# Matmuls on zeros in TensorE's idle time at the start of a fused recurrence and highway layer

## The chip, the cores and the metric

The kernel runs on one core of a Trainium2 chip. The metric is the device time of one execution in microseconds (us), the median over several runs. The core has five engines that run side by side: TensorE (PE in the profile, its weight loads PEld), VectorE (DVE), ScalarE (ACT), GpSimd (POOL) and SyncE (SP), which here only issues DMAs.

## The reference

The inputs are x and f_logit, 4 x 6336 x 256 in float32, and the weights of a highway layer of width 256. A gated recurrence runs along the 6336 steps of each batch, and its result passes the highway layer, token by token:

```python
sig = 1.0 / (1.0 + np.exp(-f_logit))
f = lower_bound + (1.0 - lower_bound) * sig
i = 1.0 - f
for t in range(S):
    h = f[:, t] * h + i[:, t] * x[:, t]
    y[:, t] = h

H = np.maximum(y @ w_h, 0.0)
T = 1.0 / (1.0 + np.exp(-(y @ w_t + b_t)))
out = T * H + (1.0 - T) * y
```

## The kernel before

The 25344 tokens are cut into 25 units: 24 of 1024 tokens of one batch and a last one that holds the rest of all four batches. A unit has eight blocks of 128 tokens. The front part of a unit (up to the recurrence) is worked in pieces, `fronts`. The first unit is cut into pieces of two, two and four blocks, the second, the third and the last into four and four; the others are one piece. The back part (the highway layer) is worked in `backs`, mostly whole units.

For the recurrence the channels must lie on the partitions and time along the row, so the front part transposes. Each step has a letter:

- L and X load a piece of f_logit (tile `lt`) and of x (tile `xt`), both issued by SP. Q loads the weights.
- U (ACT, L154) makes `u`, the sigmoid of minus f_logit, with tokens on partitions.
- P (POOL, L160) multiplies u by x into `bv`, two blocks at a time.
- A (PE, L198) transposes u into PSUM (`uT`), one 128x128 matmul a block and half of the channels. F (ACT, L205) makes the decay `f` of it, one half of the channels at a time.
- B (PE, L215) transposes bv into PSUM (`bT`), two packed bf16 values as one float32.
- S (DVE, L230) is the scan of one half of the channels over the piece, the recurrence itself. It writes `y`, from which the next piece of the same batch continues.
- W (DVE, L148) scales the weights into `w_sb`, once, in two halves.

The back part: Z and G (PE, L245) are the two products of y with the weights, `zp` and `gp`; T (ACT, L251) is the sigmoid of zp, D (DVE, L256) the maximum; E (DVE, L166) and H (POOL, L160) multiply the two into `e`; O (PE, L296 and L297) brings the sum back to tokens on partitions; C (ACT, L303) and V (DVE) copy it out of PSUM into `o`; R (SP) stores it.

The order of all this work is one string, `PLAN`, written out by hand. The loop at the end takes letter after letter and issues that step's next instance; after A, B, Z, G and O a digit names the PSUM slot. Every instruction is pinned to this order on its engine, so each engine works its own list strictly in order, and semaphores join the lists. Transposes (A and B) share two PSUM slots of one bank each, one0 and one1. Z, G and O share three slots of two banks each, two0, two1 and two2. A step whose slot is still being read waits for the reader.

Before the plan starts, DVE waits for the small load of `lb` (lower_bound), makes the constants cc and ncc (L135, L137) and, with identity matrices that POOL builds, some diagonal matrices. TensorE has nothing to do until the first u is there.

The plan before begins as follows. Its first A is the first instruction of TensorE.

```python
"XLLLXXLXLQQUUA0A1PFFFUFUB0PSSB1A0FFPSSPB1A0XLLXLXXPFUFSSWWPB1A0G0Z1PFFUPSSDPXLLXLB0A1G2Z0..."
```

Of the kernel before, what the change touches and what calls it, by code (L numbers as in the profile page):

```python
# [11 lines left out]
FP32 = mybir.dt.float32  # L12
BF16 = mybir.dt.bfloat16
# [6 lines left out]
def kernel(  # L20
# [16 lines left out]
    nc = tc.nc  # L37
    B, S, D = x.shape
    assert D == 256
    P = 128  # L40
    NH = D // P
    NB = 8
# [37 lines left out]
    singles = ctx.enter_context(tc.tile_pool(name="singles", bufs=1))  # L80
# [4 lines left out]
    def new(key, shape, dtype):  # L85
        return pools[key].tile([P, *shape], dtype, tag=key, name=key)

    def pin(ins):
        return tc.keep_in_program_order(ins)
# [12 lines left out]
    def load(i, name, src):  # L102
        u, j0, j1 = fronts[i]
        np_, j = units[u][0], run(fronts[i])
        t = fs[i][name] = new(name, [NB, D], FP32)
        pin(nc.sync.dma_start(t[:np_, :j1 - j0].rearrange("p (k j) d -> p k (j d)", j=j), tokens(src, u, j0, j1, j)))
# [6 lines left out]
    def shape(piece):  # L113

        u, j0, j1 = piece
        return units[u][0], j1 - j0

    lb = singles.tile([P, NH], FP32, name="lb")
    bt = singles.tile([P, NH], FP32, name="bt")
# [4 lines left out]
    def load_weights(k):  # L124
        pin(nc.sync.dma_start(w_raw[:, 1 - k], (moe_w_t, moe_w_h)[k].rearrange("(h p) o -> p h o", p=P)))
# [25 lines left out]
    def gate(i):  # L151
        np_, nb = shape(fronts[i])
        u = fs[i]["u"] = new("u", [NB, D], FP16)
        pin(nc.scalar.activation(u[:np_, :nb], fs[i]["lt"][:np_, :nb], AF.Sigmoid, scale=-1.0))  # L154
# [13 lines left out]
    def product(i, k, mul):  # L168
        np_, _ = shape(fronts[i])
        if "bv" not in fs[i]:  # L170
            fs[i]["bv"] = new("bv", [NB // 2, D, 2], BF16)
        mul(inner(fs[i]["bv"][:np_, k:k + 1])[:, 0], fs[i]["u"][:np_, 2 * k:2 * k + 2],
            fs[i]["xt"][:np_, 2 * k:2 * k + 2])
# [9 lines left out]
    def psum(slot, shape, key, dtype):  # L183
        tag = ("one" if dtype in (FP16, BF16) else "two") + slot
        return ps1.tile([P, *shape], dtype, tag=tag, name=key)
# [126 lines left out]
    def each(pieces, count):  # L312
        return [(i, k) for i, piece in enumerate(pieces) for k in range(count(piece))]

    def halves_of(pieces):
        return each(pieces, lambda p: len(halves(p)))
# [7 lines left out]
    kinds = {  # L324
        "L": (lambda i, _: load(i, "lt", f_logit), each(fronts, lambda p: 1)),
        "X": (lambda i, _: load(i, "xt", x), each(fronts, lambda p: 1)),
        "Q": (lambda i, k: load_weights(k), [(0, 0), (0, 1)]),
        "U": (lambda i, _: gate(i), each(fronts, lambda p: 1)),
        "P": (lambda i, k: product(i, k, gpsimd_mul), [p for p in products if p not in EARLY]),
        "p": (lambda i, k: product(i, k, vector_mul), [p for p in products if p in EARLY]),  # L330
        "A": (decay_pe, halves_of(fronts)),
        "F": (decay_act, each(fronts, lambda p: NH)),
# [14 lines left out]
    }  # L347

    PLAN = (
        "XLLLXXLXLQQUUA0A1PFFFUFUB0PSSB1A0FFPSSPB1A0XLLXLXXPFUFSSWWPB1A0G0Z1PFFUPSSDPXLLXLB0A1G2Z0PUTFFTPPB1S"  # L350
        "SDUSSEZ1A0G0G2A1DDPFTFFPPZ1A0B1O0O2PSSTFECCUB0Z1B1G0G2SDSDA0Z0TUFTPPPPPPA0G1B1FXLLLXRRXLXDESA0Z0Z2O1"
        "UFTCTB0G0A1O1O2SDPPPFCCB1A0Z1G0O2FTUCB0G1PPPHPSDSEDPA1Z0Z2B0O1FTUCTESA1G0G1B0DDHPPPPSZ2O0O1FUTCCB1SA"
        "0G2Z0B1FDUTPHPPSXXLRLRRRLRXLRRZ1A0G2O0PDTFCEEG1B1A0O2O0UFCCDSG1B0A1Z2Z0SDPHPPPPFTTA1B0O2O1G0HPSFCCZ2"
        "B1A0Z1DUTFTEG0O2PSPLXXRXRRRRDPPHCB1SA0O1G0Z2B1FCUTDEPSG1Z0A0O2FTCPDPPHB1A0Z1G0O2SFTCDEB0Z1A1G0PLLXRR"
        "RRSDPPPUFTO2B0A1Z0G1SHDCFTEO2B0G0Z1A1PPPPCUFTSDHO2B0A1G0Z1SCFTO2B0A1DEPSZ1G0PPPCUFTDHO2B0A1O0G1SCFCD"
        "EZ2B0A1Z0PSTFTPPPG1B1O2A0O0DUCFCSG1Z2A1B0HDELXLLRXRLLRXRRRRRXPSTFPPZ1G0O2B1DTCSZ1G2A0O0PHUFTCDEB1A0G"
        "2Z1O0PSPFTCDPPHB0G1G2A1Z0UFTSA0B1FDEDSPO1O0Z2B0PPCCTPHSO1A1G0Z2B0UFTCDEPSA1G0Z2O1PPDB0FTCSA1Z2G0O1PH"
        "FUCTDELXRRXXRRLRLXXRRRA1B0G0Z1PSFTO2DCB1A0G1Z0O2PPPHSUFCTDEB1A0Z1G2O0PSDFTCB0A1Z1G2SFPPPHDO0B1A0G2ET"
        "UCFPSO1PZ0CDTB1A0Z1G2SFTUHO0A0B1DFG1EPPPPSO2A0CCZ0DFB1O2Z1B0TCUTSESHPPG0A1Z2G1DDRRRRRRRRFFTA1B0O2Z0Z"
        "1FCFSEHTTG2B1G0O1RSDDCO2SRHCZ0G1STRO2TDDEZ0CTERTG1O2O0DVDVCO2CREVO1CRO0RCVRR"  # L360
    )
    assert all(PLAN.count(k) == len(places) for k, (_, places) in kinds.items())
    todo = {k: iter(places) for k, (_, places) in kinds.items()}
    letters = iter(PLAN)
    for k in letters:
        kinds[k][0](*next(todo[k]), *([next(letters)] if k in "ABZGO" else []))
# [1 line left out]
_INS = ['x', 'f_logit', 'lower_bound', 'moe_w_h', 'moe_w_t', 'moe_b_t']  # L368
# [26 lines left out]
```

## Time and profile before

| | us |
|---|---|
| median of 6 runs | 214.68 (214.33 to 214.90) |
| the profiled execution, its own time | 214.64 |
| its span, first to last instruction | 212.9 |
| first matmul starts | 6.71 |
| first scan starts | 9.34 |
| busy: PE, DVE, ACT, POOL | 188.1, 195.3, 193.7, 160.8 |

The profile is of one execution. Its span leaves 1.7 us of the execution's own time outside. Times in its views count from the span's start. A timeline row gives start, duration, engine, line, operation, output and inputs, shape and count; in brackets stands how long the engine had idled before and what ended that. Matmuls are pipelined and each row of them contains the time for the last result to arrive, so the pace of a group is read from the starts. The page's slices are a fortieth of the span each, 5.3 us, and their digits are busy tenths. The row PEclk is the clock that the throttle granted to TensorE.

### The profile page before, as it was taken

The page shows a single profiled execution, that of the slowest core. Times are in us where ns is not written, and L with a number is a line of the kernel's source. Part 1 is how long each engine was busy: PE and PEld are TensorE (multiplying, and loading weights), DVE is VectorE, ACT ScalarE, POOL GpSimd, SP SyncE. Part 2 cuts the span into 40 slices and gives each one's busy share as a digit, 9 for nine tenths or more (in the row PEclk, how much of TensorE's full clock was granted, in tenths as well). Part 3 has the DMA queues.
Part 4 walks back from the last instruction along what each step waited for, and adds up shares of the span by engine and source line. Part 5 has one row for each costly group of instructions (what it writes and reads, how often), then busy time and mean ns, then how long its engine had stood idle before and what let it go on. Part 6 is the DMA issues. An engine that isn't in the chain of part 4 may idle for free.

```text
span 212.9 us, 4616 instructions
## 1 busy us (share of the span) xinstructions
PE 188.1 (88%) x1800; PEld 131.9 (62%) x1800; DVE 195.3 (92%) x154; ACT 193.7 (91%) x194; POOL 160.8 (76%) x133
## 2 busy tenths in 40 slices
PE   0368988899898999999999999999999999999980
PEld 0245655468565767666766776668576676866770
DVE  1269999999999999999999999999999999999980
ACT  2757899999999999999999999999999999998750
POOL 4485745979499698978988988898898886866500
PEclk9999999999999999999999999999999999999997
DMA  4999999999999999999999999999999996252466
GB/s 96 402 411 431 422 426 428 423 422 422 422 422 416 423 420 423 430 420 416 428 420 426 423 426 425 424 410 427 417 429 405 357 394 258 85 213 99 195 250 200
DMA packets 17350, 78.69 MB, mean 370 GB/s; under 512 B 2352, under 2 KB 2864, under 8 KB 11952
## 3 DMA queue, kind: packets, MB, share of 16 engines
q1 hardware_dynamic: 16784, 78.39, 90.3%
q8 instruction: 14, 0.23, 0.4%
q10 hardware_dynamic: 544, 0.00, 0.1%
q14 instruction: 8, 0.07, 0.1%
HBM read 52.43 MB, written 25.95 MB: 368 GB/s over the span
## 4 chain that ended last, share of the span: by engine, by line
DMA 41%; ACT 20%; PE 18%; DVE 9%; issue 8%; POOL 1%; SPq 1%; ACTq 1%; DVEq 0%; POOLq 0%
DMA out_dram<-o 19%; DMA xt<-in_x_dram 18%; ACT t L251 6%; ACT u L154 5%; PE zp L245 5%; ACT f L205 5%; DMA lt<-in_f_logit_dram 4%; PE gp L245 4%; DVE d L256 4%; DVE y L230 4%; ACT o L303 4%; PE bT L215 3%; PE uT L198 2%; PE op L296 2%; PE op L297 1%
## 5 line engine op out<-in xcount | busy, mean ns | idle before, releaser
L160 POOL TENSOR_TENSOR bv<-u,xt 128x512 bf16<-128x512 f16 (+1 forms) x100 | 114.5, 1177 | 32.2 <-DVE e L166 10.3
L230 DVE TENSOR_TENSOR_SCAN y<-f,y,bT 128x1024 bf16<-128x1024 f16 (+3 forms) x56 | 106.5, 1919 | 2.9 <-ACT f L205 1.3
L205 ACT ACTIVATE f<-uT,ncc 128x1024 f16<-128x1024 f16 (+3 forms) x60 | 66.0, 1111 | 2.5 <-PE uT L198 2.5
L251 ACT ACTIVATE t<-zp,bt 128x1024 bf16<-128x1024 f32 (+1 forms) x52 | 63.8, 1249 | 1.0 <-PE zp L245 0.7
L256 DVE SCALAR_TENSOR_TENSOR d<-y,ncc,gp 128x1024 bf16<-128x1024 bf16 (+1 forms) x52 | 62.4, 1210 | 0.3 <-issue 0.2
L245 PEld LDWEIGHTS <-w_sb 128*128 128x128 f16 x400 | 38.0, 99 | 37.6 <-issue 5.8
L303 ACT COPY o<-op 128x1024 f32<-128x1024 f32 (+2 forms) x50 | 55.7, 1158 | 4.2 <-PE op L297 2.2
L154 ACT ACTIVATE u<-lt 128x2048 f16<-128x2048 f32 (+3 forms) x30 | 53.3, 1780 | 5.2 <-DMA lt<-in_f_logit_dram 5.2
L245 PE MATMUL zp<-y,w_sb 128*128 128x512 bf16 (+1 forms) x200 | 51.3, 382 | 1.0 <-DVE d L256 0.6
L245 PE MATMUL gp<-y,w_sb 128*128 128x512 bf16 (+1 forms) x200 | 51.3, 382 | 0.8 <-ACT t L251 0.2
L296 PE MATMUL op<-diag,y 128*128 128x128 f16 (+1 forms) x400 | 49.2, 219 | 1.9 <-DVE d L256 0.7
L160 POOL TENSOR_TENSOR e<-d,t 128x1024 bf16<-128x1024 bf16 x21 | 44.9, 2136 | 7.4 <-DVE e L166 2.6
L297 PE MATMUL op<-ident_b,e 128*128 128x128 bf16 (+1 forms) x400 | 49.2, 219 | 0.0
L297 PEld LDWEIGHTS <-e 128*128 128x128 bf16 (+1 forms) x400 | 44.8, 114 | 5.6 <-issue 3.4
L296 PEld LDWEIGHTS <-y 128*128 128x128 bf16 (+1 forms) x400 | 44.8, 114 | 2.7
L198 PE MATMUL uT<-ident_h,u 128*128 128x128 f16 (+1 forms) x400 | 32.1, 226 | 10.0 <-ACT u L154 7.2
L198 PEld LDWEIGHTS <-u 128*128 128x128 f16 (+1 forms) x400 | 27.3, 101 | 17.1 <-ACT u L154 7.5
L215 PE MATMUL bT<-ident_f,bv 128*128 128x128 f32 (+1 forms) x200 | 32.5, 285 | 5.1 <-DVE y L230 2.4
L215 PEld LDWEIGHTS bT<-ident_f,bv 128*128 128x128 f32 (+1 forms) x200 | 23.2, 146 | 11.8 <-issue 4.7
L166 DVE TENSOR_TENSOR e<-d,t 128x1024 bf16<-128x1024 bf16 (+2 forms) x26 | 19.0, 736 | 0.1
L230 DVE TENSOR_TENSOR_SCAN y<-f,bT 128x512 bf16<-128x512 f16 (+2 forms) x8 | 10.5, 1337 | 3.8 <-PE bT L215 3.8
L135 DVE TENSOR_SCALAR cc<-lb 128x2 f32<-128x2 f32 x1 | 0.2, 169 | 4.5 <-DMA lb<-in_lower_bound_dram 4.5
(19 smaller groups left out, 10.9 us busy)
## 6 DMA issues: line engine op xcount, KB each, us to landing
out_dram<-o SPq DMA_DIRECT2D x48, 512.0 KB, 13.5
lt<-in_f_logit_dram SPq DMA_DIRECT2D x21, 1024.0 KB, 14.7
xt<-in_x_dram SPq DMA_DIRECT2D x21, 1024.0 KB, 15.2
lt<-in_f_logit_dram SPq DMA_DIRECT2D x5, 512.0 KB, 8.1
xt<-in_x_dram SPq DMA_DIRECT2D x5, 512.0 KB, 8.2
lt<-in_f_logit_dram SPq DMA_DIRECT2D x2, 384.0 KB, 13.1
xt<-in_x_dram SPq DMA_DIRECT2D x2, 384.0 KB, 11.3
xt<-in_x_dram SPq DMA_DIRECT2D x2, 256.0 KB, 5.0
```

Source lines behind the costliest of these rows:

```text
L154: pin(nc.scalar.activation(u[:np_, :nb], fs[i]["lt"][:np_, :nb], AF.Sigmoid, scale=-1.0))
L160: ins = pin(nc.gpsimd.tensor_mul(out_, a, b))
L198: pin(nc.tensor.transpose(uT[:, j * np_:(j + 1) * np_], fs[i]["u"][:np_, j, h * P:(h + 1) * P], ident_h[:np_, :np_]))
L205: pin(nc.scalar.activation(f[:, :N].rearrange("p (k q j) -> p k q j", q=np_, j=j), fs[i]["uT", h].rearrange("p (k j q) -> p k q j", q=np_, ...
L215: pin(nc.tensor.transpose(t[:, k // r, k % r], fs[i]["bv"][:np_, k, h * P:(h + 1) * P].rearrange("p d j -> p (d j)").bitcast(FP32), ident_ ...
L230: pin(nc.vector.tensor_tensor_scan(y, fs[i]["f", h][:, c:c + w], fs[i]["bT", h][:, c:c + w], 0.0 if prev is None else prev, op0=ALU.mult, ...
L245: pin(nc.tensor.matmul(p[:, a:e], w_sb[:, k, ki, h * P:(h + 1) * P], y_of(j)[:, ki, a:e], start=ki == 0, stop=ki == NH - 1))
L251: pin(nc.scalar.activation(bs[j]["t"][:, m, :width(backs[j])], bs[j]["zp", m], AF.Sigmoid, bias=bt[:, m:m + 1]))
L256: pin(nc.vector.scalar_tensor_tensor(bs[j]["d"][:, m, :width(backs[j])], y_of(j)[:, m], ncc[:, m:m + 1], bs[j]["gp", m], op0=ALU.mult, op1 ...
L296: pin(nc.tensor.matmul(o, y[:, h, cols], diag[:, h], start=True, stop=False))
L297: pin(nc.tensor.matmul(o, bs[j]["e"][:, h, cols], ident_b, start=False, stop=True))
L303: pin(copy(bs[j]["o", q][:np_, a:e], bs[j]["op", q][:np_, a:e]))
```

## The change

A tile `filler` of 128x512 bf16 is set to zero by DVE ahead of all else. A new letter M in the plan stands for one matmul of 128x512 that takes its weights and its moving data from filler and writes into a PSUM tile `busy`, which takes slot two2 ahead of that slot's other users. Nobody reads busy. 22 letters M are put into the head of the plan: 11 before the first A, one after each of the first two A, four after the first B, and five before the third B. All other letters keep their order, and so does every engine's list of the other instructions.

```diff
+    filler = singles.tile([P, 512], BF16, name="filler")
+    nc.vector.memset(filler, 0.0)
 
     lb = singles.tile([P, NH], FP32, name="lb")
...
-        "XLLLXXLXLQQUUA0A1PFFFUFUB0PSSB1A0FFPSSPB1A0XLLXLXXPFUFSSWWPB1A0G0Z1PFFUPSSDPXLLXLB0A1G2Z0PUTFFTPPB1S"
...
+        "XLLLXXLXLQQUUMMMMMMMMMMMA0MA1PFFFUFUMB0PSSMMMMB1A0FFPSSPMMMMMB1A0XLLXLXXPFUFSSWWPB1A0G0Z1PFFUPSSDPXL"
+        "LXLB0A1G2Z0PUTFFTPPB1SSDUSSEZ1A0G0G2A1DDPFTFFPPZ1A0B1O0O2PSSTFECCUB0Z1B1G0G2SDSDA0Z0TUFTPPPPPPA0G1B1"
...
+    assert set(PLAN) <= {*kinds, *"M012"}
     assert all(PLAN.count(k) == len(places) for k, (_, places) in kinds.items())
     todo = {k: iter(places) for k, (_, places) in kinds.items()}
+    busy = psum("2", [NB * P], "busy", FP32)
     letters = iter(PLAN)
     for k in letters:
+        if k == "M":
+            pin(nc.tensor.matmul(busy[:, :512], filler[:, :P], filler, start=True, stop=True))
+            continue
         kinds[k][0](*next(todo[k]), *([next(letters)] if k in "ABZGO" else []))
```

More of the change, by code (lines that the diff above doesn't have):

```diff
@@ L349 @@
     PLAN = (
-        "XLLLXXLXLQQUUA0A1PFFFUFUB0PSSB1A0FFPSSPB1A0XLLXLXXPFUFSSWWPB1A0G0Z1PFFUPSSDPXLLXLB0A1G2Z0PUTFFTPPB1S"
[L351 to L359, printed above, removed]
@@ L360 @@
-        "1FCFSEHTTG2B1G0O1RSDDCO2SRHCZ0G1STRO2TDDEZ0CTERTG1O2O0DVDVCO2CREVO1CRO0RCVRR"
+        "XLLLXXLXLQQUUMMMMMMMMMMMA0MA1PFFFUFUMB0PSSMMMMB1A0FFPSSPMMMMMB1A0XLLXLXXPFUFSSWWPB1A0G0Z1PFFUPSSDPXL"
+        "LXLB0A1G2Z0PUTFFTPPB1SSDUSSEZ1A0G0G2A1DDPFTFFPPZ1A0B1O0O2PSSTFECCUB0Z1B1G0G2SDSDA0Z0TUFTPPPPPPA0G1B1"
+        "FXLLLXRRXLXDESA0Z0Z2O1UFTCTB0G0A1O1O2SDPPPFCCB1A0Z1G0O2FTUCB0G1PPPHPSDSEDPA1Z0Z2B0O1FTUCTESA1G0G1B0D"
+        "DHPPPPSZ2O0O1FUTCCB1SA0G2Z0B1FDUTPHPPSXXLRLRRRLRXLRRZ1A0G2O0PDTFCEEG1B1A0O2O0UFCCDSG1B0A1Z2Z0SDPHPPP"
@@ new lines @@
+        "PFTTA1B0O2O1G0HPSFCCZ2B1A0Z1DUTFTEG0O2PSPLXXRXRRRRDPPHCB1SA0O1G0Z2B1FCUTDEPSG1Z0A0O2FTCPDPPHB1A0Z1G0"
+        "O2SFTCDEB0Z1A1G0PLLXRRRRSDPPPUFTO2B0A1Z0G1SHDCFTEO2B0G0Z1A1PPPPCUFTSDHO2B0A1G0Z1SCFTO2B0A1DEPSZ1G0PP"
+        "PCUFTDHO2B0A1O0G1SCFCDEZ2B0A1Z0PSTFTPPPG1B1O2A0O0DUCFCSG1Z2A1B0HDELXLLRXRLLRXRRRRRXPSTFPPZ1G0O2B1DTC"
+        "SZ1G2A0O0PHUFTCDEB1A0G2Z1O0PSPFTCDPPHB0G1G2A1Z0UFTSA0B1FDEDSPO1O0Z2B0PPCCTPHSO1A1G0Z2B0UFTCDEPSA1G0Z"
+        "2O1PPDB0FTCSA1Z2G0O1PHFUCTDELXRRXXRRLRLXXRRRA1B0G0Z1PSFTO2DCB1A0G1Z0O2PPPHSUFCTDEB1A0Z1G2O0PSDFTCB0A"
@@ L361 @@
+        "1Z1G2SFPPPHDO0B1A0G2ETUCFPSO1PZ0CDTB1A0Z1G2SFTUHO0A0B1DFG1EPPPPSO2A0CCZ0DFB1O2Z1B0TCUTSESHPPG0A1Z2G1"
+        "DDRRRRRRRRFFTA1B0O2Z0Z1FCFSEHTTG2B1G0O1RSDDCO2SRHCZ0G1STRO2TDDEZ0CTERTG1O2O0DVDVCO2CREVO1CRO0RCVRR"
     )
+    assert set(PLAN) <= {*kinds, *"M012"}
     assert all(PLAN.count(k) == len(places) for k, (_, places) in kinds.items())
     todo = {k: iter(places) for k, (_, places) in kinds.items()}
+    busy = psum("2", [NB * P], "busy", FP32)
     letters = iter(PLAN)
     for k in letters:
+        if k == "M":
+            pin(nc.tensor.matmul(busy[:, :512], filler[:, :P], filler, start=True, stop=True))
+            continue
```

## The prediction

> **What bounds the kernel now.** I read the page's busy times and slices first, to see which engine has no room and where.
>
> ```profile
> PE 188.1 (88%) x1800; PEld 131.9 (62%) x1800; DVE 195.3 (92%) x154; ACT 193.7 (91%) x194; POOL 160.8 (76%) x133
> ...
> PE   0368988899898999999999999999999999999980
> ...
> DVE  1269999999999999999999999999999999999980
> ACT  2757899999999999999999999999999999998750
> ...
> PEclk9999999999999999999999999999999999999997
> DMA  4999999999999999999999999999999996252466
> ```
>
> VectorE (DVE) and ScalarE (ACT) are full from about slice 5 (5.3 us each) to slice 37. By windows, DVE is busy 35.90 of 36 us in 24 to 60, 49.33 and 49.94 of 50 in the next two stretches, 30.00 of 30 in 160 to 190; ACT has 35.54, 50.00, 50.00 and 30.00. So the end is: the moment at which both begin to run without a gap, plus fixed work, plus a short tail. DMA is also full to slice 33, but it is then at 2 to 6 tenths while DVE and ACT are still full: it has room at the end, they have not. Only the ramp, up to about 25 us, can give anything. The second view is who waited for whom there, DVE in 0 to 24 us:
>
> ```profile
> DVE y L230 <- PE bT L215: 4.5, 2, 3.8
> DVE cc L135 <- DMA lb<-in_lower_bound_dram: 4.5, 1, 4.5
> DVE y L230 <- ACT f L205: 1.3, 1, 1.3
> DVE y L230 <- issue: 0.5, 1, 0.5
> ```
>
> The columns are total us, times, longest. After the constants DVE waits four times, each time before a scan (L230), for a transposed input. The third view is the timeline of TensorE and DVE (start, duration, operation):
>
> ```profile
> 10.48 0.69 PE L215 MATMUL bT<-ident_f,bv 128*128 128x128 f32 x2 [1.25 <-POOL bv L160]
> 10.97 1.06 PE L198 MATMUL uT<-ident_h,u 128*128 128x128 f16 x8
> 12.80 1.08 PE L215 MATMUL bT<-ident_f,bv 128*128 128x128 f32 x4 [0.78 <-DVE y L230]
> ...
> 16.58 1.09 PE L215 MATMUL bT<-ident_f,bv 128*128 128x128 f32 x4 [1.62 <-DVE y L230]
> 17.46 1.06 PE L198 MATMUL uT<-ident_h,u 128*128 128x128 f16 x8
> 18.31 1.91 PE L245 MATMUL gp<-y,w_sb 128*128 128x512 bf16 x4
> 20.02 1.91 PE L245 MATMUL zp<-y,w_sb 128*128 128x512 bf16 x4
> 21.73 0.76 PE L215 MATMUL bT<-ident_f,bv 128*128 128x128 f32 x4
> 22.32 0.61 PE L198 MATMUL uT<-ident_h,u 128*128 128x128 f16 x8
> 22.77 1.03 PE L245 MATMUL gp<-y,w_sb 128*128 128x512 bf16 x4
> ...
> 13.98 2.45 DVE L230 TENSOR_TENSOR_SCAN y<-f,y,bT 128x512 bf16<-128x512 f16 x2 [1.32 <-ACT f L205]
> ...
> 22.58 2.45 DVE L230 TENSOR_TENSOR_SCAN y<-f,y,bT 128x512 bf16<-128x512 f16 x2 [0.53 <-issue]
> ```
>
> The same four matmuls gp take 1.91 us at 18.31 and 1.03 us at 22.77; eight uT take 1.06, then 0.61. TensorE runs at half speed to about 22 us. The row PEclk reads 9 there: it does not record this state, the durations do. From the starts, one 128x512 matmul is 0.43 us cold and 0.215 warm, one uT 0.11 and 0.055, one bT 0.22 and 0.11. Cold TensorE has gaps, yet two late scans wait for it.
>
> **The change part by part.** It adds one DVE memset, 22 matmuls (M) with 22 weight loads, and a PSUM tile. The order of every other instruction on all five queues is the same; no wait is added to a real instruction except that it follows the M's on TensorE.
>
> *The memset.* At the head of DVE's queue. Nearest rows: 0.28 us for a DVE operation on 128x128, 0.20 for a POOL memset of 128x128. I take 0.3 us. DVE idles until 4.45 us for lb, which covers it: cost nothing. The first M can start near 1.1 us.
>
> *The PSUM tile* shares slot two2, whose first real user is the gp at 22.77, after the last M: nothing.
>
> *The first 11 M.* Cold, 11 x 0.43 = 4.7 us, from 1.1 to 5.8. The first uT starts at 6.71, when its u is ready: 0.9 us of room, cost nothing, warm or cold.
>
> *Single M after each of the first two uT groups.* 0.43 us cold. The first ends before 7.80. The second moves bT from 8.57 by 0.1 if cold, by nothing if warm.
>
> *4 M before the bT at 10.48.* TensorE idles 1.25 us there, for POOL. Warm 0.86 us: covered. Cold 1.7 us: 0.3 late.
>
> *5 M before the bT at 12.80.* Warm: bT 10.48 to 10.7, eight uT 0.45 to 11.2, M 1.08 to 12.2: covered, since bT needs the product that POOL ends at 12.8. Cold: uT to 12.1, M 2.15 to 14.2: bT 1.4 us late.
>
> *What a warm TensorE gives.* (a) Four bT at 12.80 take 0.60 us, not 1.08: the scan at 13.98 starts at 13.5. The row names ACT f for that wait, but f for this scan is the first of two from 12.65 (0.68 us, so 13.3); the second belongs to the next scan, and bT ended at 13.88, the same moment. Gain 0.44 to 0.48 us; 0 if the named engine is right. (b) From there DVE has no gap up to 22.05: two scans, two w_sb, two scans, one d. For its next scan (22.58) bT stands behind gp and zp on TensorE. Warm, these two need 1.72 us instead of 3.42. The second half of gp must await w_sb at about 18.2, so gp and zp end near 19.5, and bT (its products are ready at 19.7) near 20.3, where DVE comes to it at 21.6. The 0.53 us go. (c) The first two scans start 0.2 earlier, but the next gap swallows that, because POOL's product waits for its xt transfer. Sum on DVE: 0.46 + 0.53 = 1.0 us.
>
> ACT must come along. Its f at 14.99 waited 1.10 us and its f at 18.56 waited 1.36 us for uT; zp cost it 0.26 and 0.46 more. Warm: the uT at 13.95 saves 0.43, bT plus uT before 18.56 save another 0.45, zp more: ACT gains over 1.3 us by 25 us, more than DVE. Do transfers allow it? By the landing records the lt of the pieces after 12 us land 1.4 us or more before their u starts (14.14 for 15.58; 17.99 for 19.71), and the o buffers come free 2.1 us or more before the copy that needs them. POOL's products wait for xt until 24.35, but their scans follow 2 us or more after the products end. So 1.0 us passes; what is late next is again the scan itself. The profiled run's own time is 214.64 (span 212.9 and 1.7 around it), by 0.04 under the median of 214.68: 214.64 - 1.0 = 213.6.
>
> [...] The row: the first full-speed matmuls are those near 22 us, after gp and zp had run without a gap from 18.31; the transposes from 10.48 to 18, TensorE busy about half the time, did not release the clock. [...] The trace shows no such drop in mid-kernel, but there TensorE is never less than 70% used. At the end it stops at 206.9; the granted clock of 0.88 in 200 to 213 means half speed for 3.1 us, thus from 209.8. I take the middle: the first 11 mostly suffice, and the transposes mostly hold the clock, because from 12 to 17 us there are still two groups of bT and two of uT, 0.45 us each when warm, about a third of the time[...].
>
> **The rivals.**
> *1. Warm early, lost again before gp.* [...] Against it: transposes are matmuls on the same array. Gain (a) only, less if the drop comes before 13 us: 214.2 to 214.6.
> *2. Warm too late: the M's block a cold TensorE (slower).* The place is the 5 M before the bT at 12.80. If TensorE is cold to that point, bT goes 1.4 us later, the scan at 13.98 and everything after it on DVE too; 0.53 comes back at 22.58, where DVE no longer waits. +0.8: 215.4. It decides when the clock opens after about 12.8 us; at 13.5 it is a draw. [...] Against it: from 7.8 us cold M's and transposes fill TensorE nearly without a gap[...].
> *3. No effect because transfers set the pace.* DMA is full to slice 33 and is 41% of the chain. Against it: ACT waited for lt only three times, 5.2 us, all before 12 us. Time 214.6.
>
> **How the numbers follow.** Warm by 11 us and held: 0.50, at 213.6 (213.3 to 213.9). Rival 1: 0.20, half of it beyond the bound. Rival 2 with its draws: 0.24, of which 0.19 slower. Rival 3: 0.06. About 0.2% (0.43 us) is what a measurement of this kernel tells from no change, so faster means under 214.25. Faster 0.60, same 0.20, slower 0.20. The range, 213.3 to 215.0, leaves out the full price of rival 2 and little else. [...] single times should scatter more than the 0.57 us of before.
>
> **What would show it.** Right: gp at about 17.3 to 18.2 with four in about 1.03; four bT near 12.8 in 0.60; the DVE waits of 1.3 and 0.5 at 0.9 and none; from 30 us on the same rows about 1 us earlier. Wrong: M's at 0.43 us beyond 10 us; a bT that starts near 14 right behind M's; gp again at 1.91; or the ramp earlier and the end not.

## The result, and the profile after

The changed kernel took 213.10 us (median of 16 runs, 212.71 to 214.17). The kernel before, run beside it on the same chip, took 214.51 (35 runs, 213.57 to 215.79). The ratio is 0.9941, with a 95% interval from 0.9925 to 0.9957: a gain of 0.9 to 1.6 us. The profiled execution took 212.87 us with a span of 211.1, against 214.64 and 212.9, so 1.8 us less. Times of the kernel before differ a little between chips (medians of 213.82 to 214.56 in the groups below), so every ratio here is to its runs on the same chip.

The page first, then who waited for whom on DVE in 0 to 24 us.

```profile
PE 190.7 (90%) x1822; PEld 131.2 (62%) x1822; DVE 195.1 (92%) x155; ACT 193.8 (92%) x194; POOL 160.8 (76%) x133
...
PE   7559888899889999999999999999999999999970
...
DVE  1379999999999999999999999999999999999980
```

```profile
DVE y L234 <- PE bT L219: 4.6, 3, 3.0
DVE cc L139 <- DMA lb<-in_lower_bound_dram: 3.6, 1, 3.6
DVE filler L120 <- PEq L388: 0.9, 1, 0.9
```

The busy times of DVE and ACT are as before: no work went away, it only starts earlier. DVE now waits ahead of three scans instead of four, and all three wait for bT. The wait of 0.5 us ahead of the scan that was at 22.58 is gone. The 1.3 us ahead of the scan that was at 13.98, put down to f before, are now 1.15 us and put down to bT. Next, rows of TensorE and DVE in the ramp.

```profile
1.19 4.06 PE L373 MATMUL busy<-filler 128*128 128x512 bf16 x11 [1.19 <-DVE filler L120]
...
10.70 1.24 PE L373 MATMUL busy<-filler 128*128 128x512 bf16 x5
12.04 0.91 PE L219 MATMUL bT<-ident_f,bv 128*128 128x128 f32 x4
...
16.78 1.03 PE L249 MATMUL gp<-y,w_sb 128*128 128x512 bf16 x4
17.64 1.03 PE L249 MATMUL zp<-y,w_sb 128*128 128x512 bf16 x4
```

```profile
13.05 2.45 DVE L234 TENSOR_TENSOR_SCAN y<-f,y,bT 128x512 bf16<-128x512 f16 x2 [1.15 <-PE bT L219]
15.42 1.39 DVE L152 SCALAR_TENSOR_TENSOR w_sb<-o,cc 128x512 f16<-128x512 f32 x2
16.72 2.33 DVE L234 TENSOR_TENSOR_SCAN y<-f,bT 128x512 bf16<-128x512 f16 x2
...
20.13 2.45 DVE L234 TENSOR_TENSOR_SCAN y<-f,y,bT 128x512 bf16<-128x512 f16 x2
```

TensorE comes to full speed within the first block: eleven M's at 0.43 us each would take 4.7 us and take 4.06, and the granted clock in the trace changes at 4.29. The five M's at 10.70 take 1.24, and the first gp and zp take 1.03 each instead of 1.91. DVE runs from 13.05 without a gap. Against the same rows before, its scans start earlier by 0.93 (13.98 to 13.05), then 1.84 (18.56 to 16.72), then 2.45 us (22.58 to 20.13). The forecast had 1.0 in all. Of the first step, 0.51 belongs to this execution: an xt that landed earlier (12.38, against 12.89). The second step, 0.9 us between two scans, is a term that the forecast doesn't have. It is the operation between them, w_sb, whose two halves took 2.29 us before and take 1.39 now. The next fence has these rows: w_sb before and POOL's product before, then POOL's product after.

```profile
16.35 2.29 DVE L148 SCALAR_TENSOR_TENSOR w_sb<-o,cc 128x512 f16<-128x512 f32 x2
16.92 2.74 POOL L160 TENSOR_TENSOR bv<-u,xt 128x512 bf16<-128x512 f16 x2 [1.59 <-DMA xt<-in_x_dram]
```

```profile
16.39 2.56 POOL L164 TENSOR_TENSOR bv<-u,xt 128x512 bf16<-128x512 f16 x2 [1.57 <-ACT f L209]
```

Before, w_sb started at 16.35 and POOL's product joined at 16.92. The view of w_sb by itself gives shortest, median and longest of the two halves: 724, 1185 and 1646 ns before, 727, 737 and 747 after. So the half that ran beside POOL took more than twice as long, and POOL's pair took 2.74 us where it elsewhere takes 2.29. After, w_sb is through at 16.81 and meets only the first 0.4 us of the product. The row of the product names f, but in every profile except those of e4 and f4, whose edits delay it, that product starts 0.16 us after its xt has landed (16.23 here, 16.76 before): its start is set by the load.

The ends of the operations show more than a slowdown: the one that starts second ends at a fixed distance after the end of the first, as if it had waited for it. That it waits is the author's reading of these distances; no row names such a wait. Before, POOL's first product ended at 18.09 and the second half of w_sb 0.55 us after it (18.64); POOL's second product, begun at 18.05, ended 1.02 us after w_sb (19.66). The other profiles have the same two distances wherever w_sb and a product overlap by more than 0.1 us: 0.54 to 0.55 us, and 1.02 to 1.03.

The 2.45 us do not reach the end. By 25 us ACT does the same work 2.5 us earlier than in the profile before (this is called its lead below), and with it comes to the loads too early:

```profile
32.52 1.91 ACT L158 ACTIVATE u<-lt 128x2048 f16<-128x2048 f32 x1 [0.42 <-DMA lt<-in_f_logit_dram]
```

This u had 2.9 us of room before (lt landed at 31.56, u started at 34.43). ACT's lead is 1.9 us from there on. The load did not come earlier with the work but later (32.44). The next two loads land when they did before (34.86 and 39.72, against 34.75 and 39.62), so they are only 0.47 and 0.40 us ahead of their u, 2.5 and 2.4 before. A copy to o at 138.61 starts 0.08 us after the store that frees its buffer has landed (2.7 us of room before); this costs no lead here. DVE's lead falls to that of ACT: 2.1 us at 44 (an e beside a POOL product took 0.2 more than before), 2.0 at 77, 1.8 at 186.

### The profile page after: what moved, and what is told of

It reads as the page before. It is cut to its first block, busy times and chain, and to the rows that moved or that the text cites. A ratio compares the mean times of both kernels' runs of the same rounds, so it can differ in the third digit from the quotient of the medians.

```text
span 211.1 us, 4661 instructions
## 1 busy us (share of the span) xinstructions
PE 190.7 (90%) x1822; PEld 131.2 (62%) x1822; DVE 195.1 (92%) x155; ACT 193.8 (92%) x194; POOL 160.8 (76%) x133
## 4 chain that ended last, share of the span: by engine, by line
PE 37%; ACT 34%; issue 11%; DVE 7%; DMA 5%; POOL 1%; SPq 1%; ACTq 1%; DVEq 0%; POOLq 0%
ACT t L255 11%; PE zp L249 10%; ACT f L209 9%; PE gp L249 9%; ACT u L158 7%; ACT o L307 7%; PE op L300 5%; PE op L301 5%; PE uT L202 4%; DVE y L234 4%; PE bT L219 4%; DMA xt<-in_x_dram 3%; DMA out_dram<-o 3%; DVE d L260 2%; POOL bv L164 1%
## 5 line engine op out<-in xcount | busy, mean ns | idle before, releaser
L209 ACT ACTIVATE f<-uT,ncc 128x1024 f16<-128x1024 f16 (+3 forms) x60 | 63.5, 1074 | 1.4 <-PE uT L202 1.4
L255 ACT ACTIVATE t<-zp,bt 128x1024 bf16<-128x1024 f32 (+1 forms) x52 | 61.5, 1201 | 0.3 <-DVE e L170 0.3
L307 ACT COPY o<-op 128x1024 f32<-128x1024 f32 (+2 forms) x50 | 53.4, 1106 | 4.1 <-PE op L301 2.0
L158 ACT ACTIVATE u<-lt 128x2048 f16<-128x2048 f32 (+3 forms) x30 | 51.8, 1732 | 5.1 <-DMA lt<-in_f_logit_dram 5.0
L249 PE MATMUL zp<-y,w_sb 128*128 128x512 bf16 (+1 forms) x200 | 50.4, 376 | 0.9 <-DVE d L260 0.6
L219 PE MATMUL bT<-ident_f,bv 128*128 128x128 f32 (+1 forms) x200 | 31.5, 276 | 4.7 <-DVE y L234 1.6
L202 PE MATMUL uT<-ident_h,u 128*128 128x128 f16 (+1 forms) x400 | 30.4, 218 | 4.9 <-ACT f L209 2.4
L202 PEld LDWEIGHTS <-u 128*128 128x128 f16 (+1 forms) x400 | 25.9, 98 | 12.5 <-issue 5.7
L219 PEld LDWEIGHTS bT<-ident_f,bv 128*128 128x128 f32 (+1 forms) x200 | 22.1, 141 | 12.2 <-POOL bv L164 5.0
L373 PE MATMUL busy<-filler 128*128 128x512 bf16 x22 | 7.1, 462 | 1.2 <-DVE filler L120 1.2
```

Source lines behind the costliest of these rows:

```text
L202: pin(nc.tensor.transpose(uT[:, j * np_:(j + 1) * np_], fs[i]["u"][:np_, j, h * P:(h + 1) * P], ident_h[:np_, :np_]))
L209: pin(nc.scalar.activation(f[:, :N].rearrange("p (k q j) -> p k q j", q=np_, j=j), fs[i]["uT", h].rearrange("p (k j q) -> p k q j", q=np_, ...
L219: pin(nc.tensor.transpose(t[:, k // r, k % r], fs[i]["bv"][:np_, k, h * P:(h + 1) * P].rearrange("p d j -> p (d j)").bitcast(FP32), ident_ ...
L249: pin(nc.tensor.matmul(p[:, a:e], w_sb[:, k, ki, h * P:(h + 1) * P], y_of(j)[:, ki, a:e], start=ki == 0, stop=ki == NH - 1))
L255: pin(nc.scalar.activation(bs[j]["t"][:, m, :width(backs[j])], bs[j]["zp", m], AF.Sigmoid, bias=bt[:, m:m + 1]))
L307: pin(copy(bs[j]["o", q][:np_, a:e], bs[j]["op", q][:np_, a:e]))
```

## The experiments

There are two questions: which part of the M's does the work, and where did the 1.4 us of lead beyond the forecast come from and part of it go. The clock is read in two ways: from durations, and from the mean granted clock of a run, which does not show the cold start (it is 0.993 for the kernel before, cold to 22 us), but does show a clock that was granted and lost again. In the profiles with a lost stretch it was 0.960 to 0.990, in those without 0.991 to 0.996, so a mean under 0.99 is counted below as a lost clock.

**e1: only the first eleven.**

```diff
-        "XLLLXXLXLQQUUMMMMMMMMMMMA0MA1PFFFUFUMB0PSSMMMMB1A0FFPSSPMMMMMB1A0...
+        "XLLLXXLXLQQUUMMMMMMMMMMMA0A1PFFFUFUB0PSSB1A0FFPSSPB1A0...
```

> Only the 11 matmuls ahead of the first transposes are kept; the other 11 M are gone. Theory 1 (the first block opens the clock, and transposes and gp hold it): uT and bT stay at warm pace from 6.7 us on, the scan near 13, w_sb ahead of POOL's product, median within 0.3 us of the changed kernel (213.1 to 213.4). Theory 2 [...]: the clock opens near 4 to 7 us and is lost by 9 to 14 us; bT x4 near 13 takes 1.0 again and gp 1.9; median 214.0 to 214.6.

Measured: 213.94 us, ratio 1.0001 (0.9987 to 1.0014). The windows of TensorE (stretch, length, busy time and count, granted clock, DMA share, GB/s) and one row of its timeline:

```profile
4.70:8.00 3.30, 1.50 (x12) 1.00 0.89 323
8.10:21.70 13.60, 9.55 (x45) 0.50 1.03 420
21.80:30.00 8.20, 7.64 (x59) 1.00 1.02 426
```

```profile
12.46 1.09 PE L219 MATMUL bT<-ident_f,bv 128*128 128x128 f32 x4 [0.78 <-DVE y L234]
```

The clock opens at 4.67 us, within the block of eleven (it takes 4.25 us, not 4.7), and is taken back from 8.08 us to 21.73 (granted 0.50). The mean clock was under 0.98 in 13 of 14 runs. Without the later M's there is no gain.

**e2: only the later eleven.**

```diff
-        "XLLLXXLXLQQUUMMMMMMMMMMMA0MA1PFFF...
+        "XLLLXXLXLQQUUA0MA1PFFF...
```

> Only the 11 M between the transposes are kept; the first block is gone. Theory 1 (the first block is what opens the clock): TensorE is cold when the 5 M come, bT that belongs at 12.8 starts 0.5 to 1.4 us late behind them, the clock opens between 11 and 15 us, median 214.3 to 215.3, not faster than the kernel before by more than 0.2 us. Theory 3 (any dense work before 12 us is as good): bT near 12.8 not late, median 213.0 to 213.4.

Measured: 213.28 us, ratio 0.9980 (0.9958 to 1.0003), single times from 212.74 to 215.59.

```profile
12.08 1.40 PE L373 MATMUL busy<-filler 128*128 128x512 bf16 x5
13.32 0.60 PE L219 MATMUL bT<-ident_f,bv 128*128 128x128 f32 x4
```

The M's and the transposes between them fill TensorE from 6.99 us on, and the clock opens at 12.40: the five M's take 1.40 us, where 0.43 each would be 2.15. In the profiled execution bT comes late (13.32), its scan starts at 14.02, and w_sb falls beside POOL's product again (2.30 us). It took 214.00. The other executions took 212.74 to 215.59; that they differ in when the clock opened is likely but not shown, since they have no profile. The interval reaches no change, and it overlaps that of the changed kernel (f1 below) as well. So the later M's alone may give the gain in many executions, and what the first block seems to add is that it comes more evenly.

**e3 and f2: five more M's after the third bT.** The longest stretch without an M or a product, from 13 to 16.8 us, is filled too.

```diff
-        ...FFPSSPMMMMMB1A0XLLXLXXPFUF...
+        ...FFPSSPMMMMMB1A0MMMMMXLLXLXXPFUF...
```

> The changed kernel with 5 more M behind the A that follows the third B, where TensorE idles 1.6 us. Theory 2 (the clock is at times lost between 12 and 17 us, since only transposes run there): gp and zp are warm in every execution, the median falls by 0.2 to 0.5 us under that of the changed kernel (212.6 to 212.9) and the scatter narrows from 1.5 us to under 0.8. Theory 1 (the transposes hold the clock anyway): same as the changed kernel, 213.1, with the same scatter.

> The changed kernel with 5 more M behind the A that follows the third B. Theory 2: no run with a mean granted clock under 0.989, median 0.2 to 0.4 us under the changed kernel beside it. Theory 1: same clock groups and same median as the changed kernel.

Measured: e3 213.06 us, ratio 0.9957 (0.9937 to 0.9977), all 8 clocks at 0.990 or more. f2, the same kernel on another chip, 213.26 us, 0.9958 (0.9943 to 0.9972), but here 6 of 22 clocks under 0.99; in its profile (214.10 us) the clock was lost from 8.36 to 11.78, ahead of the five M's, the scan was late, and w_sb fell beside POOL's product:

```profile
16.40 2.36 DVE L152 SCALAR_TENSOR_TENSOR w_sb<-o,cc 128x512 f16<-128x512 f32 x2
```

The five M's do not help the median beyond what the changed kernel has (f1 below, on the chip of f2).

**e4: the kernel before, with POOL's product held until w_sb is done.** It does alone what the change did by its timing.

```diff
+        scaled.append(pin(nc.vector.scalar_tensor_tensor(w_sb[:, :, h], ...
...
+        if hold:
+            port.append(scaled[1])
...
-            fs[i]["xt"][:np_, 2 * k:2 * k + 2])
+            fs[i]["xt"][:np_, 2 * k:2 * k + 2], **({"hold": True} if (i, k) == (4, 0) else {}))
```

> The kernel before, with no M; POOL's first product of the fifth piece (L160 in the kernel before, 16.92 us) waits for both w_sb operations of DVE, so that they do not run side by side. Theory A (part of the change's gain is that w_sb moved ahead of that product: 1.65 us beside it, 0.74 alone): the two w_sb take 1.4 us instead of 2.3, the scan at 18.56 comes 0.9 earlier, some of it is lost again to cold bT at 22.58, median 0.4 to 0.9 us under the kernel before (213.6 to 214.1). Theory B (all gain comes from TensorE's pace, the long w_sb is chance): w_sb as before, median 214.5 or, with the product 0.8 us later, up to 0.3 above.

Measured: 213.77 us, ratio 0.9998 (0.9982 to 1.0014). DVE's timeline:

```profile
16.59 1.39 DVE L150 SCALAR_TENSOR_TENSOR w_sb<-o,cc 128x512 f16<-128x512 f32 x2
18.01 2.33 DVE L234 TENSOR_TENSOR_SCAN y<-f,bT 128x512 bf16<-128x512 f16 x2
...
23.05 2.45 DVE L234 TENSOR_TENSOR_SCAN y<-f,y,bT 128x512 bf16<-128x512 f16 x2 [1.28 <-PE bT L219]
```

The median shows no gain, where theory A had 0.4 to 0.9 us. The profile is of the slowest of the 14 executions (215.34), so only its order of work is read here. w_sb takes the short time, and the next scan starts 1.42 us after w_sb began instead of 2.21. Then bT stands behind the cold gp and zp, and DVE waits 1.28 us at 23.05 where it waited 0.53. So the time that w_sb saves is lost 5 us later while TensorE is cold.

**f4: POOL beside w_sb on purpose.** The kernel of f2, with two more products on POOL (their result is not used) ahead of the product that follows w_sb.

```diff
+        if (i, k) == (3, 1):
+            for _ in range(2):
+                mul(junk[:, :].rearrange("p (a d) -> p a d", d=D), fs[i]["u"][:, 2 * k:2 * k + 2], fs[i]["xt"][:, 2 * k:2 * k + 2])
```

> The kernel with 5 more M, and two more POOL products of the same size (result unused) behind those of the fourth piece, 14.8 to 17.1 us, beside DVE's two w_sb at 15.5. Theory A (a w_sb beside a POOL product takes 0.9 us longer): the w_sb pair takes 2.2 to 3.0 us instead of 1.4, the scan behind it and all DVE work to 30 us is 0.8 to 1.6 later, the extra POOL products are stretched to 1.3 us or more; median 0.4 to 1.0 us higher. Theory B (it does not matter what POOL does): w_sb 1.4 us, median within 0.2 us.

Measured: 213.76 us, ratio 0.9983 (0.9972 to 0.9995), 0.5 us over f2 on the same chip. Rows of DVE and POOL:

```profile
16.20 2.68 DVE L153 SCALAR_TENSOR_TENSOR w_sb<-o,cc 128x512 f16<-128x512 f32 x2
...
15.59 2.73 POOL L165 TENSOR_TENSOR junk<-u,xt 128x512 bf16<-128x512 f16 x2
```

The distance is there again: w_sb ends at 18.88, 0.56 us after the second extra product. That this costs 0.5 in the median and not 1.3 has two likely reasons: f2 itself has the long w_sb in some executions, as its profile shows, and part of a larger lead is given back anyway, as the next runs show. The edit also moves POOL's next product from 17.05 (f2's profile) to 18.29. In this profile no scan waits for that, but in executions with the short w_sb one may, so the 0.5 us need not be the price of w_sb alone.

**f1: the changed kernel again.**

> The changed kernel again, as the neighbour of the next three on one chip. All theories: about 0.6% under the kernel before on this chip. Theory 2 (the clock is at times lost between 12 and 17 us): the mean granted clock of its runs falls in two groups, 0.990 to 0.997 and 0.977 to 0.988, and the second group is 0.3 us or more slower. Theory 1: the times do not follow the clock.

Measured: 213.17 us, ratio 0.9958 (0.9941 to 0.9975). In 11 of 14 runs the mean clock was under 0.99. The profile, one such run: windows of TensorE, and its timeline.

```profile
6.50:16.60 10.10, 6.48 (x47) 1.00 1.04 415
16.70:20.10 3.40, 3.18 (x14) 0.50 1.03 424
```

```profile
17.82 1.49 PE L249 MATMUL gp<-y,w_sb 128*128 128x512 bf16 x3 [0.22 <-PE uT L202]
19.10 1.53 PE L249 MATMUL zp<-y,w_sb 128*128 128x512 bf16 x4
```

The clock was lost from 16.69 to 20.10 us (0.50 in the fence), just before gp, as the first rival has it. w_sb still kept its 1.39 us (at 15.66). DVE's lead was 1.60 us at the fourth scan and did not grow by the 0.6 of the fifth; 1.3 of it was left at 171, and the execution took 213.35. So the 0.9 us of w_sb do not need the fifth scan's 0.5 to pass: here TensorE was warm up to 16.69 and began gp earlier (17.82, against 18.55 in e4). In the result above, 9 of the 16 means were under 0.99, with a median of 213.53 us; the other seven, to which its profile belongs, have 213.02. In f1 it is 213.35 and 213.10. So a lost clock costs some 0.2 to 0.5 us in these two groups, if the means sort the executions rightly.

**f3: the load of f_logit for the ninth piece one place earlier in SP's queue.** The kernel of f2, with the waiting load ahead of its x.

```diff
-        ...FFUPSSDPXLLXLB0A1G...
+        ...FFUPSSDPLXLXLB0A1G...
```

> The kernel with 5 more M, and the two loads of the ninth piece exchanged in SP's queue (lt ahead of xt), so that its lt lands about 2.4 us earlier and its xt as much later. Theory C (once TensorE is warm, the gain at 22 us is cut from 2.4 to 1.9 us by ACT's u that waits for this lt at 32.5): u of the ninth piece starts near 32.0 with no idle time ahead of it, the next two u are then within 0.1 us of their landings, and the median is 0.1 to 0.5 us lower. Theory D (what is given back is lost elsewhere): no gain, within 0.1 us.

Measured: 213.18 us, ratio 0.9953 (0.9937 to 0.9969), no better than f2. In its profile the u near 32 us no longer waits, and DVE keeps a lead of 2.5 us to 77. ACT's one wait on a transfer beyond 22 us is then here:

```profile
139.01 1.01 ACT L307 COPY o<-op 128x1024 f32<-128x1024 f32 x1 [0.81 <-DMA out_dram<-o]
```

The lead is 1.9 after it and 1.4 at 186. Here one transfer was mended, and part of the lead was taken at the next.

**g1 and g2: the store that frees this buffer goes ahead of a load**, in the changed kernel and in the kernel before.

```diff
-        ...HDELXLLRXRLLRXRRRRRXPST...
+        ...HDELXLLRXRLRLXRRRRRXPST...
```

> The changed kernel with one exchange in SP's queue, far behind the ramp: the store that is issued at 125.6 us in the changed kernel goes ahead of the lt load that waits before it for ACT's u. Theory C (the gain of the ramp is cut by transfers; at 138.6 us ACT's copy waits for this store to free its buffer): the store is issued near 118 us, lands before 134 us, the copy near 138.4 waits for nothing, and the shift of ACT against the kernel before is the same after 140 us as ahead of it; median 0.1 to 0.4 us lower than without the exchange (ratio to the kernel before 0.993 to 0.995). Theory D (nothing is given back there): ratio as without it, 0.994 to 0.996.

> The kernel before with the same exchange in SP's queue. Theory C: its copy there has 2.7 us of room after the store's landing, so the wait is one that only the gain in the ramp exposes: no difference, ratio 0.999 to 1.001. Theory D' (the store's place is worth something by itself): ratio below 0.998.

Measured: g1 213.32 us, 0.9951 (0.9938 to 0.9965); g2 214.37, 0.9992 (0.9974 to 1.0010). In g1's profile that copy starts at 138.52, 2.8 us after the store landed, and ACT's lead is the same 1.8 us on both sides of it. The median of g1 shows no gain beyond its interval; 18 of its 22 clocks were under 0.99. In the kernel before, the order makes no difference that these runs can tell.

**g3 and g4: fourteen M's in the first block**, with the five of e3 and the load of f3; g4 has g1's exchange as well.

```diff
-        "XLLLXXLXLQQUUMMMMMMMMMMMA0MA1PFFF...
+        "XLLLXXLXLQQUUMMMMMMMMMMMMMMA0MA1PFFF...
```

> The kernel with 5 more M and the two exchanged loads of the ninth piece, and 14 instead of 11 M in the first block, so that it lasts 6.0 us cold. Theory 2' (the clock opens at the end of a fixed 3.41 us stretch that is at least about 0.86 full, and is lost at the end of one that is at most 0.36 full): the block now always holds such a stretch, the clock opens before 7.2 us and no stretch up to 9 us is under 0.41, so no run has a mean granted clock under 0.989; times scatter less. Median 212.7 to 213.1 where the kernel before is at 214.1. Theory 1 (the number of M does not matter): the same groups of runs as with 11, median 213.2.

> The last kernel and the exchange of store and load together. Theory C: with neither the ninth piece's lt nor that store in the way, the 2.4 us that ACT and DVE are ahead at 25 us stay to the end where the ramp went well: profile shift near -2.2 us at 190 us, median 0.4 to 0.9 us under the kernel with the loads alone exchanged (212.0 to 212.7 where the kernel before is at 214.1). Theory D: other transfers take the gain back as well, median within 0.2 us of the kernel without the store's exchange.

Measured: g3 213.31 us, 0.9954 (0.9942 to 0.9966); g4 213.27, 0.9943 (0.9925 to 0.9962). No clock of the 29 was under 0.99: as far as the mean shows, it is now held in every execution, and yet the time is that of the changed kernel. The 0.4 to 0.9 us that theory C expected of g4 did not come. In g3's profile DVE leads by 2.39 us at the fifth scan and by 1.37 at 34, with no wait between. It is two long operations, e (about 1.2 us each in other profiles), and POOL's products beside them:

```profile
25.97 1.51 DVE L170 TENSOR_TENSOR e<-d,t 128x2048 bf16<-128x2048 bf16 x1
...
32.14 1.95 DVE L170 TENSOR_TENSOR e<-d,t 128x2048 bf16<-128x2048 bf16 x1
```

```profile
25.23 7.78 POOL L164 TENSOR_TENSOR bv<-u,xt 128x512 bf16<-128x512 f16 x6 [2.70 <-ACT u L158]
```

An xt landed at 25.07, where it landed between 23.6 and 24.5 in 14 of the 17 profiles of this document, so POOL's products started late and ran in one block beside DVE's e.

**h1, h2 and h3: the changed kernel, fourteen and five M's with no load moved, and that with g1's exchange,** on one chip.

> The changed kernel as it is, for comparison on this chip. Theory A (the clock is lost in part of the executions, and that costs the median): 0.994 to 0.997 of the kernel before, with a mean granted clock under 0.99 in many runs. Theory B (transfers cap the gain whatever the clock does): the same, and h2 no faster.

> 14 M's in the first block and 5 more after the third bT, no load moved. Theory A: no run with a mean granted clock under 0.99, a scatter of at most 0.6 us, and a median 0.2 to 0.4 us under h1. Theory B: the clocks as A has them, but the median within 0.15 us of h1, because the u of the ninth piece waits for its load near 32 us and the copy near 139 us for its store.

> h2 with one store ahead of one load near 125 us in SP's queue. Theory A and B alike: the copy near 139 us waits no longer. If the wait there costs time (0.2 to 0.5 us by the profiles in which it showed): 0.2 to 0.5 us under h2. If the gain has been given back at the load near 32 us already: within 0.1 of h2.

Measured: h1 213.41 us, 0.9942 (0.9921 to 0.9963), h2 213.36, 0.9944 (0.9922 to 0.9965), h3 213.18, 0.9934 (0.9912 to 0.9957). h2 has no mean under 0.99 and scatters by 0.44 us only, but its median is that of h1, as theory B has it. The two waits by which theory B explained this are not in h2's profile: its u at 32.88 starts 0.66 us after its load, its copy at 139.11 0.61 us after the store. What the profile shows is the collision of g3 without any load moved, so the exchange of f3 is not its cause. The xt lands at 24.92, POOL's product starts at 25.08, and e, beside it, takes 2.18 us. In h3's profile (212.60 us, the fastest of that kernel) xt lands at 23.99 and e takes 1.32.

```profile
26.26 2.18 DVE L170 TENSOR_TENSOR e<-d,t 128x2048 bf16<-128x2048 bf16 x1
25.08 2.29 POOL L164 TENSOR_TENSOR bv<-u,xt 128x512 bf16<-128x512 f16 x2 [2.26 <-DMA xt<-in_x_dram]
```

```profile
26.18 1.32 DVE L170 TENSOR_TENSOR e<-d,t 128x2048 bf16<-128x2048 bf16 x1
24.15 2.28 POOL L164 TENSOR_TENSOR bv<-u,xt 128x512 bf16<-128x512 f16 x2 [1.39 <-DMA xt<-in_x_dram]
```

The first fence is of h2, the second of h3. In both, e ends 1.07 us after POOL's pair (28.44 after 27.37, 27.50 after 26.43), though it had begun 1.11 us ahead of that end in h2 and 0.25 in h3.

h2's lead falls from 2.09 us to 1.11 there. h3's is 2.17 at 20 us and 2.04 at 171: with no transfer late, almost nothing is given back, and the execution is 2.04 us under the profiled one before.

The xt is late in three profiles, g3, g4 and h2, about 1 us each. All three are kernels with fourteen M's, of which only h3's profile does not have it; none of the 13 profiles of other kernels has it. So the fourteen M's may bring it about, and may pay for the clock that they hold; no run separates the two. As a median h3 is not told apart from the changed kernel: the interval of each holds the other's ratio. So no version here is shown to beat the changed one.

## Why the prediction was right or wrong, point by point

The direction and the two terms that the forecast counted, (a) and (b), were right. The step that failed is the sum over DVE between them: it left w_sb at its old 2.29 us, and the runs show 1.39, a third term of 0.9 us. The time came out at 213.1, and the range began at 213.3.

As a ratio the forecast (213.6 to 214.64, 0.9952) lies inside the measured interval, and some 0.1 us of the difference is the kernel before, 214.51 beside these runs. This nearness is partly luck: the lead in the ramp was 2.0 us and more, not 1.0, and lost clocks, transfers and POOL took back some of it, so that 1.4 are left in the median. h3's profile, where almost nothing was taken back, gives the terms cleanly.

- *Memset, PSUM tile, first M's at no cost.* Right. The memset took 0.27 us and the first M started at 1.19; the first uT started at 6.69, against 6.71.
- *Five M's before the bT covered.* Right in the changed kernel's profile (they end about 12.0, the product that bT's second pair awaits a little later). e2 shows the other side: started cold, they push bT to 13.32.
- *(a) 0.44 to 0.48 us.* Right. In h3 the third scan starts 0.66 earlier, of which 0.20 is an xt that landed earlier (12.69, against 12.89), so 0.46 is left. In the changed kernel's profile it is 0.93, of which 0.51 is that landing (12.38). The reading that the wait put down to f really ended with bT was right too: warm, it is named so.
- *"From there DVE has no gap up to 22.05: two scans, two w_sb, two scans, one d."* This is the step that failed. It took w_sb at its old duration, 2.29 us. The earlier start moves w_sb ahead of POOL's product, whose start is set by a load, and the two halves then take 1.39: a term of 0.9 us taken at nothing. The rows for it were in the profile before: two halves of one operation at 724 and 1646 ns, and a POOL pair of 2.74 us among pairs of 2.29. The operations of DVE that were held up beside a POOL product, w_sb (0.73 to 1.65 us) and e (1.2 to 2.18), take both inputs from SBUF. Operations with one input in PSUM were not held up: a scan of 128x512 without an earlier y took 1.19 to 1.22 us both beside POOL and apart from it, and d of 128x1024 took 1.26 us in the median both ways.
- *(b) 0.53 us.* Right: 0.60 in h3 and in the changed kernel's profile. With TensorE cold throughout (e4) the 0.9 do not pass either; with (b) alone lost (f1) most of them do.
- *"So 1.0 us passes."* Right for 1.0. The real lead was about 2, and the loads near 32 to 40 us, with 2.4 to 2.9 us of room before, did not land earlier with it; the first came 0.9 us later. The third rival, transfers, was weighed at 0.06 and as all or nothing. It came as a cap on part of the gain: a load at 32 us, a store near 139, an xt at 25 us, one or the other in different profiles.
- *"The first 11 mostly suffice."* Near the runs: the clock opened within the block at 4.29 us in the changed kernel's profile and at 4.67 in e1's. When it would open was the author's estimate; no view of the kernel before shows how full TensorE must be for it. In each of the 17 profiles the changes of the granted clock lie whole multiples of 3.41 us apart (4.67 and 8.08 in e1, 16.69 and 20.10 in f1, 4.29 and 209.09 in the changed kernel), so windows of that length can be laid through them; that each window decides the clock of the next is the author's reading. Their shares of TensorE's work are estimates from starts and paces. The clock opened after windows that were 0.83 (f1), 0.86 (e3) and more full, not after 0.73 (e4), 0.67 (f3) or 0.59 (before). It was held through a window of 0.41 (the changed kernel) and lost after 0.36 (h1 and f4) and less (f1, e1, f2, g1). By these estimates the loss goes with the share and not with one long gap: the longest idle stretch in f1's lost window was 1.7 us, while h1 kept the clock over one of 2.2 us from 14.23.
- *"The transposes mostly hold the clock."* Half right. The window before the loss in f1 held nothing but transposes, 0.28 of it, and in g1 0.23, so they did not hold the clock alone. But by these estimates they count like other matmuls. A window of f4 with 0.50 of M's and 0.45 of transposes opened the clock (8.52 to 11.93), and one of f3 with 0.67 of M's alone did not. The changed kernel's window from 11.12, with 0.19 of M's and 0.25 of transposes, held it, and one of f4 with 0.24 and 0.13 lost it. So in these windows the transposes count and are only too few.
- *Rival 1.* It happens in many executions (a mean clock under 0.99 in 9 of the 16 runs of the result, 11 of 14 of f1 and 5 of 7 of h1), and its price depends on when. Lost after 13 us (f1, 213.35) it takes (b) and leaves w_sb short. Lost from 8.8 to 12.2 (h1's profile, 213.83) it makes bT late, and w_sb takes 2.29 us again.
- *Rival 2.* Not seen in the changed kernel, whose slowest run is 214.17. The upper end of e2, which has no first block, is 215.59, where the rival was put at 215.4; that execution has no profile, so that it is this rival is not shown.
- *Scatter.* More was expected than the 0.57 us of before. But those six runs did not show the kernel's scatter, which is 2.2 us over 35 runs. With the change it is 1.5, over 16 runs.

What stays open: why that xt lands 1 us later in three of the four profiles with fourteen M's, and how often each of the losses falls in executions without a profile. An undisturbed gain of 2 us was seen in one profile only.

## What to carry to other kernels

Where TensorE is cold in a ramp, ask which waits end on it, and fill both the time before its first work and the gaps after. Here the first block alone gave nothing, and the gaps alone gave times from 212.74 to 215.59. When a change moves an operation in time, do not take its old duration: look what ran beside it, and compare the instances of the same shape: where the longest is twice the shortest, it may be a collision that the move ends or begins. And set the landing margins of the loads and stores against the largest gain that is possible, not the one forecast: with the DMA engines full (a share of 1.01 to 1.02 from 20 to 110 us) the loads near 32 to 40 us did not land earlier when the work moved 2.5 us earlier.

## What the runs showed of the hardware that was not expected

- The two VectorE operations here with both inputs in SBUF, w_sb and e, were held up beside a GpSimd product, and a product beside w_sb too: the one that started second ended at a fixed distance after the first. w_sb went from 0.73 to 1.65 us, e from 1.2 to 2.18, a POOL pair from 2.29 to 2.74. In all 25 cases of the 17 profiles in which an e of 128x2048 began more than 0.14 us before the end of a running product, it ended 1.07 to 1.08 us after that product. Where the xt landed at 24.92 us (h2), e took 2.18 us, and where it landed at 23.99 (h3), 1.32.
- The clock opened with matmuls on zeros alone: in e1's profile at 4.67 us, within the first eleven, which took 4.25 us where 0.43 each would be 4.7, with nothing else on TensorE before.
- In the 17 profiles the clock changed on a grid of 3.41 us. It opened after windows that were 0.83 full or more and not after 0.73; it was lost after 0.36 or less, and 0.41 kept it. Transposes are counted in. These shares are estimates from starts and paces.
- The cold start is not in the granted clock of the page (0.993 for the kernel that was cold to 22 us), while a clock that was lost after it was granted is (0.50 in the windows of e1 and f1).
